# Planning the order of a fused attention and expert kernel anew behind batch 1's scores, with a shorter gate, longer pooling matmuls and another last store

## The chip, the cores and the metric

The kernel runs on one core of a Trainium2 chip. The metric is the device time of one execution in microseconds. Five engines work side by side, each through its own queue in program order: PE (matrix multiplication; its weight loads are shown as PEld), DVE (vector), ACT (scalar and exponential), POOL (masks, and issuing the loads) and SP (issuing the stores). Results of matmuls land in PSUM, which has eight banks of 512 fp32 columns for each of 128 partitions; DVE and ACT copy them out to SBUF. DMA engines move data between SBUF and memory.

## The reference

Eight batches of 576 tokens, in two stages. The first is attention with eight heads of 64, whose keys and values are averaged over eight neighbouring tokens (72 pooled keys). Its output, 512 wide, is `x` of the second stage: four experts with their own 64-wide causal attention, of which every token keeps the two with the largest gate values.

```python
k_p = k.reshape(B, H, Sp, 8, D).mean(axis=3)
v_p = v.reshape(B, H, Sp, 8, D).mean(axis=3)
scores = scale * np.matmul(q, k_p.transpose(0, 1, 3, 2))
...
x = attn_out.transpose(0, 2, 1, 3).reshape(B, S, H * D)
logits = x @ w_gate
topk = np.argpartition(-logits, 2, axis=-1)[..., :2]
...
for e in range(4):
    q, k, v = x @ wq[e], x @ wk[e], x @ wv[e]
    scores = np.where(causal, -1e9, scale * (q @ k.transpose(0, 2, 1)))
    ye = softmax(scores) @ v @ wo[e]
    out += gate weight of e * ye        # for the tokens that chose e
```

Inputs and outputs are fp32; matmuls run on bf16 operands.

## The kernel before

Nothing is scheduled by a compiler. The string `SEQ` (from line 632) lists some 1,140 tokens, and the loop at line 705 carries them out one by one; each engine receives its instructions in that order. A token is a name, arguments, `:batch`, and optionally `@bank`, `d` (the evacuation runs on DVE, else on ACT), `p` (the store is issued by a later token). So `P_k1:2@5` multiplies batch 2's second half of key weights into bank 5, and `p_k1:2d` copies the result out on DVE.

The steps of a batch `b`, by their tokens:

- Loads (POOL, `load`, line 112). `L_k0` to `L_k2`, `L_q0` to `L_q3` and `L_v0` to `L_v2` bring keys, queries and values as bf16 into `kraw`, `qraw`, `vraw`, of which there are three sets, so batch `b + 3` reuses those of `b`. Weights are the tokens `W`; `W4` brings `wop`, the last projection.
- First stage. `PK` (line 265) pools the keys by matmuls with a constant matrix in four strips of 32 partitions side by side; `kc` and `kt` (lines 274, 280) turn the result into `kpT`. `u` turns the queries (`qT`). `E` gives the scores, and `e` (line 320) is their exponential on ACT. `PV`/`vc` pool the values. `D`, `d`, `x` form the reciprocal of the sum; `O` and `o` (DVE, line 365) the output `xT`.
- Second stage, projections. `V`/`v` (line 392) give values and gate logits, `P`/`p` (line 467) queries and keys (`qk`, 512 columns each; `t0` the 64 last tokens of all four, 256 columns).
- Gate. `g0` to `g9` (line 397): exponential on ACT, then the second largest of four logits by larger/smaller of pairs (`hi`, `lo`, two `s`, `m2`), a mask `msk`, the masked weights `W`, their sum, its reciprocal, and the product `G`.
- Second stage, scores. `S` multiplies, `s` (line 490) takes the exponential into `etb` on ACT in four tiles; tile 3, the block of the 64 last tokens, in two instructions (line 497). `a` (line 508) zeroes what lies above the diagonal, on POOL.
- Output. `B` multiplies with the values; `bz`, `bg`, `b` (line 549) divide by the sum and weight by the gate (`osc`, DVE). `T`/`t` turn the result by matmul into `oT`; for batches 2 to 5 the tokens `F` (line 584) do this by a DMA transpose issued by SP. `Y` multiplies with `wop`; `y` (line 602) copies the product to an output tile `ofin`, of which there are nine; `z` and `zs` (line 617) store it. Chunks 0 to 3 are 128 tokens each of one batch; chunk 4 holds the last 64 tokens of two batches together, and is stored in two halves, of which the last of batch 7 goes through ACT's queue. The very last projection, chunk 4 of batch 7, is made and copied in two column halves (`ya4`, `yb4`).

A token whose buffer or bank is still in use waits, and everything behind it on its engine waits too.

Of the kernel before, what the change touches and what calls it, by code (L numbers as in the profile page):

```python
# [16 lines left out]
ISEQ = mybir.AluOpType.is_equal  # L17
EXP = mybir.ActivationFunctionType.Exp
# [3 lines left out]
def kernel(  # L22
# [37 lines left out]
    HALF = TPP // 2  # L60

# [325 lines left out]
    def small(b, nm, *shape):  # L387
        if (b // 2, nm) not in at:
            at[b // 2, nm] = gtp.tile([128, NPC, *shape], FP32, name=nm, tag=nm)
        return at[b // 2, nm]  # L390
# [6 lines left out]
    def gate(b, step):  # L397
# [14 lines left out]
        elif step == 1:  # L412
            L2 = L.rearrange("p c (a b) -> p c a b", b=2)
            for nm, op in (("hi", MAXOP), ("lo", MINOP)):
                nc.vector.tensor_tensor(
                    out=tmp(nm, 2, 1), in0=L2[:, :, :, 0:1], in1=L2[:, :, :, 1:2], op=op
                )
        elif step == 2:
            for nm, src, op in (("s2", "hi", MINOP), ("s3", "lo", MAXOP)):
                nc.vector.tensor_tensor(  # L420
                    out=tmp(nm, 1), in0=got(src)[:, :, 0, :], in1=got(src)[:, :, 1, :], op=op
                )
        elif step == 3:
            nc.vector.tensor_tensor(
                out=tmp("m2", 1), in0=got("s2"), in1=got("s3"), op=MAXOP
            )
        elif step == 4:
            nc.vector.tensor_tensor(
                out=tmp("msk", E), in0=L, in1=got("m2").to_broadcast([128, n, E]), op=ISGE
            )  # L430
        elif step == 5:
            nc.vector.tensor_mul(out=tmp("W", E), in0=got("Ex"), in1=got("msk"))
        elif step == 6:
# [3 lines left out]
        elif step == 7:  # L437
# [4 lines left out]
        elif step == 8:  # L442
# [47 lines left out]
    def sb(b, bank, dve, ep, ti):  # L490
# [4 lines left out]
        if ti == 3:  # L495
            for e in range(2):
                nc.scalar.activation(
                    out=et[half(b), :, e, eo : eo + n],
                    in_=psum[half(b), bank + e, 0 : 2 * n].rearrange("p (a n) -> p a n", a=NEP),
                    func=EXP, scale=MOE_EXP_SCALE,  # L500
                )
# [90 lines left out]
    def Y(b, bank, c):  # L592
        p0 = 128 * place(b, c)
        last = (b, c) == (B - 1, 4)
# [7 lines left out]
    def y(b, bank, dve, c, half=None, later=False):  # L602
        ofin = at[b, "ofin", c] if (b, "ofin", c) in at else ofp.tile([128, DM], FP32, name="ofin", tag="ofin")
        if half is not None:
            cols = slice(256 * half, 256 * half + 256)
            copy(half == 1, ofin[:, cols], psum[:, bank ^ half, cols])
            at[b, "ofin", c] = ofin
            if (b, "half", c) not in at:
                at[b, "half", c] = True
                return  # L610
        else:
            copy(dve, ofin[:], psum[:, bank, :])
        at[b, "ofin", c] = ofin
        if not later:
            z(b, c, nc.sync)

    def z(b, c, queue):
        ofin = at[b, "ofin", c]
        if c == 4:
            for h in range(2):  # L620
                (nc.scalar if h and b == B - 1 else queue).dma_start(
                    out=out[b - 1 + h, MAIN:S, :], in_=ofin[64 * h : 64 * h + 64, :]
                )
        else:
            queue.dma_start(out=out[b, 128 * c : 128 * c + 128, :], in_=ofin[:])
# [10 lines left out]
        H1:0@0c H1:0@0c L_q1:1 H1:0@0c e21:0 e20:0 e11:0 D2:0@4 D0:0@5 L_q2:1 PV:0@6 d0:0 D1:0@7 vc:0d H1:0@0 x0:0  # L636
        c0:0d L_q3:1 d2:0 O00:0@6 d1:0 c1:0d O20:0@5 O01:0@4 o00:0 O10:0@2 x1:0 O11:0@3 o01:0 x2:0 X0:0@0 W2:0 o10:0
        X1:0 o11:0 X2:0 W3:0 c2:0d X3:0 c3:0d o20:0 P_k0:0@4 L_v0:1 h0:0 P_t0:0@5 p_k0:0d L_v1:1 P_k1:0@3 p_t0:0 L_v2:1
        PK:1@2 p_k1:0 S03:0@0 S00:0@4 kc:1 L_k0:2 S02:0@6 s03:0 s02:0 S01:0@2 kt:1d H1:0@0 L_k1:2 H1:0@0 H1:0@0 s01:0
        H1:0@0 L_k2:2 H1:0@0 u1:1 s00:0 u0:1 a02:0 E1:1@02 L_q0:2 e11:1 E0:1@46 c4:0d H1:0@4c L_q1:2 H1:0@4c e00:1  # L640
        V0:0@2 L_q2:2 V1:0@3 e01:1 a00:0 v0:0d V3:0@4 L_q3:2 v1:0d V2:0@2 e10:1 v3:0d a01:0 D1:1@3 v2:0d L_v0:2 PV:1@4
        d1:1 g1:0 E2:1@06 D0:1@2 vc:1d a03:0 x1:1 H1:0@3 L_v1:2 e20:1 g2:0 O11:1@3 e21:1 g3:0 O10:1@4 d0:1 o11:1 D2:1@5
        O01:1@6 L_v2:2 S10:0@0 x0:1 o10:1 S12:0@2 d2:1 s10:0 o01:1 S11:0@4 O00:1@7 g4:0 PK:2@6 s11:0 o00:1 L_k0:3
        O20:1@0 B01:0@1 kc:2 x2:1 B00:0@7 L_k1:3 g0:0 P_q1:1@4 o20:1 kt:2 bz00:0 bz01:0 s12:0 g5:0 L_k2:3 V2:1@0 g6:0
        g7:0 P_q0:1@6 g8:0 L_q0:3 v2:1 u1:2 p_q1:1 P_t0:1@0 a11:0 u0:2 p_q0:1 E1:2@24 L_q1:3 p_t0:1 g9:0 P_k0:1@6
        bg00:0 a10:0 e10:2 b00:0 bg01:0 L_q2:3 b01:0 V0:1@7 e11:2 p_k0:1d a12:0 E0:2@02 v0:1d B10:0@6 L_q3:3 W4:0 e01:2
        V4:1@4 bz10:0 B11:0@7 bg10:0 L_v0:3 b10:0 e00:2 PV:2@5 v4:1d D1:2@6 bz11:0 L_v1:3 P_k1:1@4 vc:2d d1:2 bg11:0
        b11:0 x1:2 E2:2@02 L_v2:3 D0:2@6 p_k1:1d e21:2 O11:2@7 O01:2@5 d0:2 O00:2@2 o11:2 O10:2@4 L_k0:4 e20:2 PK:3@3
        x0:2 o10:2 S03:1@0 S10:1@6 L_k1:4 s03:1 o01:2 s10:1 S01:1@0 o00:2 L_k2:4 V3:1@4 s01:1 kc:3 V1:1@5 L_q0:4 v3:1d
        S02:1@6 S11:1@2 v1:1 kt:3d S12:1@0 s02:1 L_q1:4 V2:2@4 u1:3 P_q1:2@5 a03:1 u0:3 s11:1 L_q2:4 P_q0:2@6 v2:2d  # L650
        s12:1 a02:1 p_q1:2d S00:1@2 L_q3:4 p_q0:2d g0:1 E0:3@04 s00:1 g1:1 L_v0:4 P_k0:2@6 g2:1 e00:3 g3:1 a12:1 g4:1
        P_k1:2@7 p_k0:2d e01:3 L_v1:4 E2:3@02 g5:1 B12:0@6 g6:1 L_v2:4 g7:1 e20:3 B02:0@4 g8:1 e21:3 bz12:0 T10:0@5
        g9:1 p_k1:2 a10:1 E1:3@02 bg12:0 t10:0d L_k0:5 b12:0 bz02:0 B12:1@5 bg02:0 e11:3 b02:0 PK:4@6 L_k1:5 bz12:1
        bg12:1 PV:3@4 b12:1 e10:3 kc:4 S00:2@2 L_k2:5 D1:3@5 vc:3d B01:1@6 s00:2 L_q0:5 kt:4d B02:1@7 T00:0@4 bz01:1
        V1:2@0 d1:3 bz02:1 L_q1:5 bg01:1 bg02:1 T02:0@1 t00:0d T01:0@2 D2:3@3 x1:3 b02:1 D0:3@5 a11:1 b01:1 O10:3@4
        d2:3 O00:3@7 t01:0d d0:3 L_q2:5 D2:2@6 v1:2d T11:0@3 V0:2@2 t02:0 o10:3 x0:3 a01:1 T12:0@5 V3:2@1 u0:4 L_q3:5
        t12:0 v0:2 O20:2@4 O01:3@5 v3:2 O11:3@0 a00:1 o00:3 t11:0 d2:2 L_v0:5 PV:4@1 o11:3 x2:2 x2:3 E0:4@26 o01:3 vc:4
        a00:2 Y3:0@0 L_v1:5 e01:4 o20:2 P_q1:3@5 y3:0dp e00:4 L_v2:5 T12:1@4 u1:4 B10:1@1 P_k1:3@0 p_q1:3 t12:1d bz10:1
        L_k0:6 bg10:1 E1:4@26 b10:1 p_k1:3 g1:2 P_t0:2@5 L_k1:6 e11:4 g2:2 V0:3@4 p_t0:2d Y2:0@0 e10:4 v0:3d Y1:0@5
        y2:0dp L_k2:6 V2:3@4 y1:0p g3:2 E2:4@26 O20:3@0 L_q0:6 v2:3d D1:4@1 e21:4 D0:4@5 o20:3 e20:4 PK:5@4 d1:4 L_q1:6  # L660
        u0:5 S02:2@2 d0:4 S10:2@6 V4:3@1 kc:5 s02:2 B11:1@5 kt:5d P_k0:3@4 v4:3 g4:2 bz11:1 a02:2 s10:2 bg11:1 b11:1
        P_t0:3@1 L_q2:6 p_k0:3d x0:4 T11:1@5 V1:3@0 a10:2 t11:1d p_t0:3 S12:2@2 u1:5 L_q3:6 x1:4 S11:2@4 O01:4@1 s12:2
        v1:3d O11:4@6 P_q0:3@7 o01:4 L_v0:6 s11:2 o11:4 S03:2@0 a12:2 O10:4@2 p_q0:3d D2:4@6 s03:2 PV:5@3 L_v1:6 d2:4
        o10:4 O00:4@4 g0:2 E2:5@06 vc:5 V3:3@5 o00:4 L_v2:6 e20:5 S01:2@2 e21:5 x2:4 v3:3d S01:3@0 a11:2 B00:1@4 s01:2
        g1:3 L_k0:7 T01:1@6 P_k0:4@5 bz00:1 t01:1d bg00:1 s01:3 b00:1 L_k1:7 E0:5@26 p_k0:4d V1:4@4 L_k2:7 e00:5 g2:3
        g5:2 P_k1:4@5 v1:4d L_q0:7 e01:5 g6:2 E1:5@02 g7:2 p_k1:4d V0:4@4 L_q1:7 e10:5 g8:2 T02:1@5 g9:2 P_q0:4@6 a01:2
# [123 lines left out]
```

## Time and profile before

| | before |
|---|---|
| time, median of 3 runs | 154.38 us (154.3 to 154.83) |
| span of the profiled execution, first to last instruction | 152.5 us |
| granted TensorE clock | 0.997 of full |
| PE busy | 140.5 us, 92% |
| ACT busy | 135.1 us, 89% |
| DVE busy | 125.9 us, 83% |
| POOL busy | 89.5 us, 59% |
| stores issued by SP | 32 of 256 KB, 7 of 128 KB, one more of 128 KB by ACT |

The profile comes from one execution. Its own time is known only as the span, which leaves out some 1.9 us around the program that the runs' times contain. A group's row gives line, engine, operation, output and inputs, shapes and count, then busy time, the mean of one instruction in ns, the idle time ahead of the group and what ended it. Busy time counts an overlap of two instructions once; the mean does not, so count times mean can exceed the busy time. A row of the timeline gives start and length in us. A row of DMA issues gives count, size of one and the median us from issue to landing. The row "DMA" shows in forty equal slices of 3.8 us how busy the DMA engines were, in tenths.

### The profile page before, as it was taken

How to read it: one execution, taken by the hardware profiler on the slowest of the kernel's cores; microseconds unless marked ns; L12 is line 12 of the kernel's file. 1: busy time of each engine (PE TensorE's matmuls, PEld its weight loads, DVE VectorE, ACT ScalarE, POOL GpSimd, SP SyncE). 2: the span in 40 equal slices, each digit the busy share in tenths (PEclk: the TensorE clock that was granted, in tenths of full speed). 3: DMA queues.
4: the chain of work that ended last, by engine and by line, in shares of the span. 5: the costliest groups of instructions: out<-in, count | busy, mean ns of one | idle time of the engine just before them, and what ended most of it. 6: DMA issues, size and time to landing. Idle time of an engine off the chain costs nothing.

```text
span 152.5 us, 5419 instructions
## 1 busy us (share of the span) xinstructions
PE 140.5 (92%) x2101; PEld 78.8 (52%) x2122; DVE 125.9 (83%) x415; ACT 135.1 (89%) x247; POOL 89.5 (59%) x161
## 2 busy tenths in 40 slices
PE   6776998999999999999999999999999999999970
PEld 2323353465554465565546655856356667546640
DVE  1784846899899899899989999999897699888960
ACT  3359479999999999999999999999999899999860
POOL 6998588999688979958998171123300344442300
PEclk9999999999999999999999999999999999999998
DMA  4999999999999999999999931536528241389994
GB/s 126 237 186 181 181 179 178 180 180 181 179 188 180 179 181 182 178 180 182 169 173 176 181 34 39 211 84 208 176 92 325 83 121 25 66 282 306 333 340 134
DMA packets 68890, 26.67 MB, mean 175 GB/s; under 512 B 62720, under 2 KB 64000, under 8 KB 68864
## 3 DMA queue, kind: packets, MB, share of 16 engines
q0 software_dynamic: 57408, 14.72, 97.2%
q1 hardware_dynamic: 11088, 10.88, 22.2%
q10 hardware_dynamic: 368, 0.72, 1.5%
q8 instruction: 16, 0.26, 0.6%
q14 instruction: 10, 0.08, 0.2%
HBM read 30.42 MB, written 9.44 MB: 261 GB/s over the span
## 4 chain that ended last, share of the span: by engine, by line
PE 66%; DVE 11%; DMA 10%; POOL 4%; ACT 3%; issue 2%; DVEq 0%; POOLq 0%
PE psum L221 65%; DMA qraw<-in_q_dram 5%; DMA wst_q<-in_moe_wq_dram 4%; DVE xT L377 4%; ACT etb L503 2%; POOL kraw L126 2%; POOL vraw L126 2%; PE psum L230 1%; DVE qT L298 1%; DVE osc L562 1%; DVE oT L212 1%; POOL qraw L126 1%; DVE vp L212 1%; DVE ofin L212 1%; ACT eta L331 1%
## 5 line engine op out<-in xcount | busy, mean ns | idle before, releaser
L503 ACT ACTIVATE etb<-psum 128x1024 bf16<-128x1024 f32 x48 | 47.2, 1032 | 0.8 <-PE psum L221 0.4
L520 POOL TENSOR_SCALAR_AFFINE_SELECT etb<-etb 128x256 bf16<-128x256 bf16 x64 | 25.7, 412 | 37.2 <-ACT etb L503 36.0
L331 ACT ACTIVATE eta<-psum 96x1024 bf16<-96x1024 f32 (+1 forms) x48 | 36.0, 802 | 1.1 <-PE psum L221 0.4
L221 PEld LDWEIGHTS <-etb 128*128 128x128 bf16 x480 | 18.0, 97 | 6.3 <-issue 3.5
L126 POOL DMA_DIRECT2D qraw<-in_q_dram x30 | 19.7, 662 | 2.5 <-DVE gt L557 0.8
L377 DVE TENSOR_TENSOR xT<-psum,rza 128x512 bf16<-128x512 f32 x32 | 20.2, 681 | 1.0 <-ACT rza L354 0.5
L221 PE MATMUL psum<-wvg,xT 128*128 128x260 bf16 x144 | 20.8, 275 | 0.1
L126 POOL DMA_DIRECT2D kraw<-in_k_dram x25 | 19.0, 765 | 2.3 <-POOLq L774 0.8
L221 PE MATMUL psum<-vaug,etb 128*128 128x65 bf16 x480 | 20.2, 193 | 0.0
L126 POOL DMA_DIRECT2D vraw<-in_v_dram x24 | 18.8, 785 | 2.3 <-PE psum L221 1.4
L221 PE MATMUL psum<-xT,wqp 128*128 128x64 bf16 (+1 forms) x123 | 19.2, 282 | 0.5 <-issue 0.2
L221 PE MATMUL psum<-xT,wkp 128*128 128x64 bf16 (+1 forms) x121 | 18.8, 281 | 0.4
L221 PE MATMUL psum<-wop,oT 128*128 128x512 bf16 (+1 forms) x67 | 17.9, 373 | 0.5 <-DVE oT L212 0.3
L212 DVE CAST qk<-psum 128x512 bf16<-128x512 f32 (+1 forms) x23 | 15.0, 653 | 3.6 <-PE psum L221 3.6
L562 DVE TENSOR_TENSOR osc<-psum,gt 128x256 bf16<-128x256 f32 (+2 forms) x40 | 16.7, 421 | 1.0
L221 PE MATMUL psum<-qk 64*128 64x64 bf16 (+4 forms) x192 | 16.2, 277 | 0.6 <-DVE xT L377 0.2
L221 PEld LDWEIGHTS <-xT 128*128 128x128 bf16 x144 | 12.6, 97 | 6.9 <-issue 3.0
L212 ACT COPY ofin<-psum 128x512 f32<-128x512 f32 (+1 forms) x25 | 14.0, 587 | 1.1 <-PE psum L221 0.9
L298 DVE STREAM_TRANSPOSE qT<-qraw 128x576 f32<-128x576 f32 (+1 forms) x18 | 13.2, 750 | 1.0 <-DMA qraw<-in_q_dram 0.9
L221 PE MATMUL psum<-qT,kpT 32*128 32x64 bf16 (+1 forms) x256 | 12.5, 289 | 1.1 <-DVE qT L298 0.9
L221 PE MATMUL psum<-eta,vp 96*32 96x512 bf16 (+1 forms) x256 | 12.7, 288 | 0.5 <-DVE vp L212 0.5
L221 PEld LDWEIGHTS <-wqp 128*128 128x128 bf16 x128 | 8.4, 97 | 8.4 <-issue 2.3
(79 smaller groups left out, 214.4 us busy)
## 6 DMA issues: line engine op xcount, KB each, us to landing
out_dram<-ofin SPq DMA_DIRECT2D x32, 256.0 KB, 2.9
vraw<-in_v_dram POOLq DMA_DIRECT2D x24, 192.0 KB, 6.7
qraw<-in_q_dram POOLq DMA_DIRECT2D x30, 144.0 KB, 7.0
kraw<-in_k_dram POOLq DMA_DIRECT2D x21, 192.0 KB, 7.5
out_dram<-ofin SPq DMA_DIRECT2D x7, 128.0 KB, 2.4
xT<-in_q_dram ACTq DMA_DIRECT2D x2, 288.0 KB, 4.7
xT<-in_k_dram SPq DMA_DIRECT2D x2, 192.0 KB, 4.9
kraw<-in_k_dram POOLq DMA_DIRECT2D x4, 96.0 KB, 5.2
```

The lines of the kernel that those rows point to most:

```text
L126: nc.gpsimd.dma_start(out=dst, in_=src)
L212: (nc.vector.tensor_copy if dve else nc.scalar.copy)(out=out, in_=in_)
L221: nc.tensor.matmul(out=out, lhsT=lhsT, rhs=rhs, start=start, stop=stop)
L230: nc.tensor.transpose(out=out[s], in_=in_[:, s], identity=ident[0:n, 0:n])
L298: nc.vector.transpose(out=dst.rearrange("p (a s n) -> p a n s", s=32, n=n)[:, :, own], in_=src.rearrange("p (a n d) -> p a n d", n=n, d=32 ...
L331: nc.scalar.activation(out=dst, in_=src, func=EXP, scale=ATT_EXP_SCALE)
L377: nc.vector.tensor_tensor(out=xT[:, 2 * got[0][0] + t : 2 * got[-1][0] + t + 1 : 2, m + got[0][1].start : m + got[0][1].stop], in0=psum[:, ...
L503: nc.scalar.activation(out=et[:, ep, :, eo : eo + n], in_=psum[:, bank : bank + 2, 0:n], func=EXP, scale=MOE_EXP_SCALE,)
L520: nc.gpsimd.affine_select(out=blk, in_=blk, pattern=[[0, 2], [1, 128]], compare_op=ISGE, fill=0.0, base=0, channel_multiplier=-1,)
L562: nc.vector.tensor_tensor(out=osc(b, ep)[:, own, :].rearrange("p c (e d) -> p e c d", e=2), in0=o[:, :, :, 0:HD], in1=gt.to_broadcast([128 ...
```

## The change

It has five parts.

1. Pooling of keys: for batches 1 to 7 the three column blocks are one matmul of 384 columns (batch 0 keeps three).
2. Gate: steps 1 to 5 become three. `ahead` compares every logit with every other (bf16 result, 4 by 4 for each token), `c1` counts how many are larger, and one fused operation keeps the exponential where fewer than 1.5 are.
3. Tile 3 of the second stage's scores: one exponential over both banks.
4. The shared chunk 4 is one store of 256 KB. The column halves move from chunk 4 to chunk 3 of batch 7 (`FINAL`), and chunk 4 becomes the last, whole.
5. The order. The tokens up to batch 1's scores are the same; behind `a02:0 E1:1@02` they stand in another order, with other banks and another choice between DVE and ACT. Loads, masks, stores and transposes are moved with it.

```diff
 def PK(b, bank, j=None):
     n = 64 * (own(j).stop - own(j).start)
-    for c in range(3):
+    for cs in [slice(c, c + 1) for c in range(3)] if b in LONG else [slice(0, 3)]:
         for t in range(2):
             for i in range(4):
-                mm(psum[32 * i : 32 * i + 32, bank, n * c : n * c + n], poolk[:, :],
-                   raw[:, c, pair(b, i)][:, own(j), t, :], start=(t == 0), stop=(t == 1))
+                mm(psum[32 * i : 32 * i + 32, bank, n * cs.start : n * cs.stop], poolk[:, :],
+                   raw[:, cs, pair(b, i)][:, :, own(j), t, :], start=(t == 0), stop=(t == 1))
...
         elif step == 1:
-            L2 = L.rearrange("p c (a b) -> p c a b", b=2)
-            for nm, op in (("hi", MAXOP), ("lo", MINOP)):
-                nc.vector.tensor_tensor(out=tmp(nm, 2, 1), in0=L2[:, :, :, 0:1], in1=L2[:, :, :, 1:2], op=op)
+            nc.vector.tensor_tensor(out=tmp("ahead", E, E), in0=L.unsqueeze(2).to_broadcast([128, n, E, E]),
+                                    in1=L.unsqueeze(3).to_broadcast([128, n, E, E]), op=ISGT)
         elif step == 2:
-            for nm, src, op in (("s2", "hi", MINOP), ("s3", "lo", MAXOP)):
-                nc.vector.tensor_tensor(out=tmp(nm, 1), in0=got(src)[:, :, 0, :], in1=got(src)[:, :, 1, :], op=op)
+            nc.vector.reduce_sum(out=tmp("c1", E), in_=got("ahead"), axis=mybir.AxisListType.X)
         elif step == 3:
-            nc.vector.tensor_tensor(out=tmp("m2", 1), in0=got("s2"), in1=got("s3"), op=MAXOP)
-        elif step == 4:
-            nc.vector.tensor_tensor(out=tmp("msk", E), in0=L, in1=got("m2").to_broadcast([128, n, E]), op=ISGE)
-        elif step == 5:
-            nc.vector.tensor_mul(out=tmp("W", E), in0=got("Ex"), in1=got("msk"))
+            nc.vector.scalar_tensor_tensor(out=tmp("W", E), in0=got("c1"), scalar=1.5, in1=got("Ex"),
+                                           op0=ISLT, op1=MULT)
...
         if ti == 3:
-            for e in range(2):
-                nc.scalar.activation(out=et[half(b), :, e, eo : eo + n],
-                    in_=psum[half(b), bank + e, 0 : 2 * n].rearrange("p (a n) -> p a n", a=NEP), ...)
+            nc.scalar.activation(out=et[half(b), :, :, eo : eo + n].rearrange("p a e n -> p e a n"),
+                in_=psum[half(b), bank : bank + 2, 0 : 2 * n].rearrange("p e (a n) -> p e a n", a=NEP), ...)
...
-        last = (b, c) == (B - 1, 4)
+        last = (b, c) == (B - 1, FINAL)
...
         if c == 4:
-            for h in range(2):
-                (nc.scalar if h and b == B - 1 else queue).dma_start(
-                    out=out[b - 1 + h, MAIN:S, :], in_=ofin[64 * h : 64 * h + 64, :])
+            queue.dma_start(out=out[b - 1 : b + 1, MAIN:S, :], in_=ofin[:])
```

The loads behind batch 2's second query load, first as before and then as after, up to batch 4:

```diff
-L_q2:2 L_q3:2 L_v0:2 L_v1:2 L_v2:2 L_k0:3 L_k1:3 L_k2:3 L_q0:3 L_q1:3 L_q2:3 L_q3:3 W4:0 L_v0:3 L_v1:3 L_v2:3 L_k0:4 ...
+L_q3:2 L_q2:2 L_k2:3 L_v1:2 L_v2:2 L_v0:2 L_k0:4 L_q2:3 L_q1:3 L_k1:3 L_k0:3 L_q0:3 L_k1:4 L_q3:3 L_v2:3 L_k2:4 ...
```

SP's queue ahead of the token `y2:2` in the new order, and the end of both orders:

```diff
+y0:3p ... zs0:3 ... zs0:0 ... zs0:2 ... F11:4 ... zs2:1 F00:4 ... Y2:2@3 ... y2:2dp
...
-T12:7@2 t02:7d zs2:7 t12:7d Y4:7@2 zs3:7 ya4:7 yb4:7d
+Y3:7@2 zs0:7 zs1:7 z2:7 t12:6d ya3:7 T02:7@5 t02:7d yb3:7d Y4:7@4 zs3:7 y4:7p zs4:7
```

More of the change, by code (lines that the diff above doesn't have):

```diff
@@ L388, in small @@
         if (b // 2, nm) not in at:
-            at[b // 2, nm] = gtp.tile([128, NPC, *shape], FP32, name=nm, tag=nm)
+            at[b // 2, nm] = gtp.tile([128, NPC, *shape], BF16 if nm == "ahead" else FP32, name=nm, tag=nm)
         return at[b // 2, nm]
@@ L436, in gate @@
             )
-        elif step == 7:
+        elif step == 5:
             nc.vector.scalar_tensor_tensor(
@@ L495, in sb @@
         if ti == 3:
-            for e in range(2):
[L497 to L501, printed above, removed]
+            nc.scalar.activation(
+                out=et[half(b), :, :, eo : eo + n].rearrange("p a e n -> p e a n"),
+                in_=psum[half(b), bank : bank + 2, 0 : 2 * n].rearrange("p e (a n) -> p e a n", a=NEP),
+                func=EXP, scale=MOE_EXP_SCALE,
+            )
         else:
@@ L606, in y @@
             copy(half == 1, ofin[:, cols], psum[:, bank ^ half, cols])
[L607 to L610, printed above, removed]
         else:
             copy(dve, ofin[:], psum[:, bank, :])
-        at[b, "ofin", c] = ofin
-        if not later:
-            z(b, c, nc.sync)
+            if not later:
+                z(b, c, nc.sync)
     def z(b, c, queue):
@@ L642 @@
[L642 to L666, printed above, removed]
```

129 lines of the change are left out of this document (74 added, 55 removed).

## The prediction

> **What bounds the kernel now.** I read the page first, then its chain of waits, then busy time by stage.
>
> ```profile
> span 152.5 us, 5419 instructions
> PE 140.5 (92%) x2101; PEld 78.8 (52%) x2122; DVE 125.9 (83%) x415; ACT 135.1 (89%) x247; POOL 89.5 (59%) x161
> DMA  4999999999999999999999931536528241389994
> PE 66%; DVE 11%; DMA 10%; POOL 4%; ACT 3%; issue 2%; DVEq 0%; POOLq 0%
> 15.00 8.13 DMA qraw<-in_q_dram
> ```
>
> The chain runs through loads until batch 1's queries land at 23.1 us; nothing ahead of that point is reordered. Behind it TensorE carries the chain. The next view splits the rest of the span; its columns are window, length, then busy us of PE, PEld, DVE, ACT and POOL.
>
> ```profile
> 36.00:60.00 24.00, 23.56 (x389) 13.08 (x387) 22.36 (x72) 23.39 (x45) 20.57 (x35) 1.00 1.79 181
> 60.00:90.00 30.00, 29.74 (x457) 15.91 (x456) 28.24 (x87) 29.48 (x56) 22.77 (x40) 1.00 1.69 167
> 90.00:120.00 30.00, 29.58 (x496) 17.94 (x499) 27.04 (x87) 29.47 (x54) 5.55 (x14) 1.00 0.48 154
> 120.00:146.10 26.10, 25.87 (x364) 16.82 (x368) 22.52 (x93) 24.90 (x49) 9.93 (x25) 1.00 0.57 181
> ```
>
> From 36 to 146 us PE idles 1.35 of 110.1 us and ACT 2.86. The two feed each other through eight PSUM banks, so both look full. How full each is shows in the next rows.
>
> ```profile
> 143.58 0.59 PE L221 MATMUL psum<-wop,oT 128*128 128x512 bf16 x2
> L221 PE MATMUL psum<-wop,oT 128*128 128x512 bf16 x63 | 17.3, 380 | 0.2
> L503 ACT ACTIVATE etb<-psum 128x1024 bf16<-128x1024 f32 x48 | 47.2, 1032 | 0.8 <-PE psum L221 0.4
> 119.35 1.94 ACT L503 ACTIVATE etb<-psum 128x1024 bf16<-128x1024 f32 x2 [0.39 <-PE psum L221]
> ```
>
> One 512-column matmul is recorded as 0.38 us, yet two take 0.59: the second starts 0.21 after the first, so up to 0.17 us of waiting behind a PE record still counts as busy. On ACT two exponentials of 1.03 take 1.94, a step of 0.91, so only 0.12 of 1.03 can hide. PE's "full" is the softer one. I take ACT, with PE close behind, as the bound from 60 us on. Before 60 us the DMA row is at 9 throughout: there the loads set the pace.
>
> **The change part by part.**
>
> *Work on ACT.* Counted over the order, these evacuations move from ACT to DVE, net of those moving back: two kpT, two 512-column qk, three 256-column qk, three 64-column oT; one 256-column oT and one ofin come back to ACT. The two 64-partition exponentials of each batch become one.
>
> ```profile
> L212 ACT CAST qk<-psum 128x512 bf16<-128x512 f32 x10 | 5.8, 590 | 0.5 <-PE psum L221 0.5
> L212 ACT CAST qk<-psum 128x256 bf16<-128x256 f32 x5 | 2.0, 408 | 0.3 <-PE psum L221 0.3
> L212 ACT CAST kpT<-kf 128x384 bf16<-128x384 f32 x2 | 1.0, 523 | 0.0
> L212 ACT COPY oT<-psum 128x256 bf16<-128x256 bf16 x5 | 1.9, 388 | 0.4 <-PE psum L230 0.4
> L212 ACT COPY oT<-psum 128x64 bf16<-128x64 bf16 x4 | 0.9, 218 | 0.0
> L212 ACT COPY ofin<-psum 128x512 f32<-128x512 f32 x24 | 13.6, 596 | 0.6 <-PE psum L221 0.4 <-ACT oT L212 0.2
> L497 ACT ACTIVATE etb<-psum 64x128 bf16<-64x128 f32 x16 | 3.5, 271 | 0.1
> L331 ACT ACTIVATE eta<-psum 96x256 bf16<-96x256 f32 x16 | 5.3, 376 | 0.1
> ```
>
> Copies: 2×0.523 + 2×0.590 + 3×0.408 + 3×0.218 − 0.388 − 0.596 = 3.1 us. Exponentials: 16×0.271 − 8×0.376 (priced by the 256-column row) = 1.3. Together 4.4 us of records in 16 fewer instructions. Each neighbour hides about 0.12 of a record, so the time freed may be as little as 4.4 − 16×0.12 = 2.5. Since ACT runs back to back, I take 2.5 and keep 4.4 for the range. About 0.5 of it lies ahead of 60 us, where loads pace the work; 2.0 is left.
>
> *Work on DVE.* It receives the copies and loses part of the gating.
>
> ```profile
> L212 DVE CAST qk<-psum 128x512 bf16<-128x512 f32 (+1 forms) x23 | 15.0, 653 | 3.6 <-PE psum L221 3.6
> L212 DVE CAST kpT<-kf 128x384 bf16<-128x384 f32 (+1 forms) x6 | 3.0, 502 | 0.1
> L428 DVE TENSOR_TENSOR msk<-L,m 128x16 f32<-128x16 f32 (+1 forms) x8 | 1.6, 201 | 0.1
> L420 DVE TENSOR_TENSOR s<-lo 128x4 f32<-128x4 f32 (+1 forms) x8 | 1.3, 158 | 0.0
> L562 DVE TENSOR_TENSOR osc<-psum,gt 128x128 bf16<-128x128 f32 x8 | 2.2, 288 | 0.2
> ```
>
> Copies add at most 5×0.653 + 2×0.502, less the ofin that leaves (0.596, ACT's row): 3.7. Seven small operations per batch (hi, lo, two s, m, msk, W) go: 56 at 0.16 to 0.20, 9 to 11.2 us. Three come back (compare of 64 or 80 elements, sum, fused threshold): 24 between the 0.201 of msk and the 0.288 of a 128-element product, 4.8 to 6.9; I take 0.25, 6.0. DVE ends between +1.6 and −2.7 us, about even. It idles 9.9 of the 110.1 us above, which covers even +1.6; without that cover this 1.6 would come off the gain.
>
> A page prices the new compare directly. The Trainium skill, "VectorE: DVE Perf Modes", section on the TRN2 errata, gives a two-input fp32 operation (N+151)/0.96 ns, 224 to 241 ns here (an estimate by that page); with it the added gating is some 5.6 us instead of 6.0 and the sum stays. The trace agrees only roughly: for 16 to 20 elements the formula gives 174 to 178 ns, msk's row 201.
>
> *Pooling matmuls.* For batches 1 to 7 twenty-four 128-column matmuls become eight of 384 columns, with as many columns streamed.
>
> ```profile
> 43.11 0.51 PE L221 MATMUL psum<-kraw,poolk 96*32 96x128 bf16 x24
> 54.30 0.40 PE L221 MATMUL psum<-vraw,poolv 96*32 96x512 bf16 x3
> ```
>
> Today 24 take 0.51. The nearest long form is one group of side-by-side strips of 512 columns, 0.40; with a second start 0.21 later, two groups take 0.61. By columns (384 of 512) that is 0.46, and if only the spacing shrinks, 0.40 + 0.16 = 0.56. So a batch gains 0.05 or loses 0.05, seven batches ±0.4. I take −0.1: as many columns are streamed and 16 weight loads fewer.
>
> *Loads.* The same 79 loads; the queue's order changes behind batch 2's second query load.
>
> ```profile
> qraw<-in_q_dram POOLq DMA_DIRECT2D x8, 144.0 KB, 7.3
> 37.90 0.66 POOL L126 DMA_DIRECT2D qraw<-in_q_dram  x1
> 46.49 1.42 DVE L298 STREAM_TRANSPOSE qT<-qraw 128x576 f32<-128x576 f32 x2
> 49.42 0.63 PE L221 MATMUL psum<-qT,kpT 32*128 32x512 bf16 x8
> ```
>
> The loading stages move 181 GB/s, so a key load of 192 KB holds the DMA engines for 1.06 us. Two such loads of batch 4 (L_k0:4, L_k1:4) now stand ahead of batch 3's last query load. That one was issued at 37.90 and landed about 7.3 later, at 45.2; with 2.1 us more ahead of it, 47.3. The two transposes that read it began at 46.49, so DVE would wait up to 0.8 there, with v2:2 and p_q0:2 queued behind. The scores that need them began at 49.42, 1.5 after the transposes ended. I price this at 0 by that cover; without it, it costs the 0.8. Two stores (zs3:0, zs2:0) enter the loading stage, near 66 us, where batch 5's loads follow; a store's 256 KB at 181 GB/s would push them 1.4 us each at most. Weights wop slip behind batch 4's loads.
>
> *Tail.* Chunk 3 of batch 7 is evacuated in halves, and the shared last tokens follow whole.
>
> ```profile
> 148.16 0.42 DVE L212 COPY ofin<-psum 128x256 f32<-128x256 f32 x1 [0.74 <-PE psum L221]
> 148.66 0.55 ACTq L621 DMA_DIRECT2D out_dram<-ofin  x1
> out_dram<-ofin ACTq DMA_DIRECT2D x1, 128.0 KB, 2.6
> out_dram<-ofin SPq DMA_DIRECT2D x1, 256.0 KB, 2.0
> out_dram<-ofin SPq DMA_DIRECT2D x32, 256.0 KB, 2.9
> ```
>
> The last copy grows from 0.42 to ACT's 0.60 for a whole tile (+0.18), the landing from issue falls from 2.6 to the 2.0 of a lone 256 KB store (−0.6), or to the page's median 2.9 (+0.3) if queued. Bounds −0.4 to +0.5; I take 0.
>
> *Sum.* −2.0 (ACT), 0 (DVE), −0.1 (pooling), 0 (loads, tail): 152.5 − 2.1 = 150.4 of span. The span lies 1.9 below the 154.38 median of three runs, so the time is 152.3.
>
> **The rivals.** *PE is the bound.* For it: PE's idle is the smaller of the two, and the chain is 66% PE. Against: its records hide up to 0.17 us each. ACT's relief is then worth nothing, only pooling's −0.4 to +0.4 counts and a little of the order: 154.2.
>
> *Loads pace longer.* For it: the DMA row stays at 9 up to 87 us. If relief counts only behind that, half of the 2.0 is lost: 153.3. Against: PE idles less from 60 to 90 us (0.26 of 30) than from 36 to 60 (0.44 of 24).
>
> *Output tiles run out (slower).* There are nine output tiles; a new one waits until the store nine before it has landed. In the new order y2:2 on DVE needs the store of y2:1, only fifteen tokens ahead, and SP gets to that one after three stores and a transpose.
>
> ```profile
> 95.58 1.55 SPq L625 DMA_DIRECT2D out_dram<-ofin  x3
> 97.22 2.13 SPq L587 DMA_TRANSPOSE oT<-osc  x1
> 106.83 1.22 SPq L590 DMA_TRANSPOSE oT<-osc  x1
> ```
>
> From y0:3's copy, which frees SP: 3×0.52 + 1.22 to 2.13 + landing 2.0 to 2.9 from the issue of y2:1's store = 4.8 to 6.6 us. ACT's work between that copy and Y2:2 is at least the four large exponentials of batch 5 (0.91 each), two small (0.27) and one qk copy (0.59), 4.8. DVE would wait up to 1.8 us, with bz11:5 and bz01:5 behind it and their PSUM banks held. Two more close pairs follow (y1:4, y3:4). It decides once the store lands more than 4.8 after that copy; two waits of the full 1.8 cost 3.6, and from the forecast 152.3 the time is 155.9. Against: 2.0-us landings are seen too.
>
> **How the numbers follow.** Forecast 152.3: 0.48, its own range 150.5 (ACT's 4.4 less 0.5 ahead of 60 us, nothing else) to 153.5 (the two bad bounds of loads and pooling, 0.8 and 0.5). Loads 0.12. PE 0.16. Output tiles 0.24. A measurement tells about 0.5% (0.8 us) from no change. Faster takes the first and most of the second, 0.58; same the third and the second's rest, 0.18; slower 0.24. The range goes from 150.5 to 155.8, which leaves no more than two in ten outside.
>
> **What would show it.** Right: ACT's busy time down by about 4 us with its share still 97% or more between 60 and 140 us; DVE's within 3 us of 125.9; a pooling group of eight in about 0.5; batch 3's query transposes near 46.5; PE's last Y4 about 2 us earlier. Wrong: DVE ofin waiting for a DMA (output tiles); ACT's share falling with PE's at 99% (PE bound); POOL waiting for ACT's etb ahead of 80 us with gaps in the DMA row, which would starve loads and make this forecast too low.

## The result and the profile after

| | before | after |
|---|---|---|
| time, median | 154.36 us (4 runs) | 171.21 us (4 runs, 170.08 to 173.02) |
| span of the profiled execution | 152.5 us | 170.9 us |
| granted TensorE clock in it | 0.997 | 0.959 |

The ratio is 1.106, interval 1.1015 to 1.1105: slower by about 16.9 us where 2.1 us of gain was forecast. Medians here and below are of all runs, while a ratio compares only those within 1.5% of the fastest run of their kernel. The profiled execution of after took 173.02 us; the spans of the other three are 167.9 to 169.3 us.

First the page of after: span, busy time, the DMA row in forty slices of 4.3 us, the chain by engine, and the median from issue to landing of the stores.

```profile
span 170.9 us, 5136 instructions
PE 146.1 (86%) x2010; PEld 78.6 (46%) x2010; DVE 122.9 (72%) x391; ACT 133.4 (78%) x231; POOL 88.7 (52%) x161
DMA  5999999999999999999997773962064557676810
PE 42%; DMA 28%; ACT 10%; DVE 6%; issue 4%; SPq 3%; POOL 1%; DVEq 0%; ACTq 0%; POOLq 0%
out_dram<-ofin SPq DMA_DIRECT2D x35, 256.0 KB, 6.5
```

ACT and DVE are busy 1.7 and 3.0 us less than before. TensorE has fewer matmuls and yet 5.6 us more of busy time. Of this, 1.5 us are there without the merged store as well (142.0 us in the run in two halves below). For the rest, its granted clock is below full in two stretches that begin near the ends of two waits: 0.50 from 114 to 116 us and 0.57 from 156.5 to 160. Why it falls there isn't shown; behind a third wait, of 2.1 us until 148.5, it stays full. The chain has 28% in DMA where it had 10%, and a store takes 6.5 us to land where it took 2.9. Next the stages of after, in the columns of the view of before (window, length, busy us of PE, PEld, DVE, ACT, POOL, then granted clock, DMA share, GB/s).

```profile
36.00:60.00 24.00, 23.71 (x342) 12.28 (x343) 22.31 (x71) 23.31 (x41) 20.54 (x35) 1.00 1.66 167
60.00:90.00 30.00, 28.98 (x428) 15.10 (x417) 26.80 (x75) 27.56 (x56) 20.54 (x35) 1.00 1.61 171
90.00:120.00 30.00, 27.71 (x424) 15.52 (x424) 23.69 (x76) 25.39 (x42) 8.54 (x20) 0.94 0.64 91
120.00:146.10 26.10, 26.10 (x370) 16.29 (x363) 21.04 (x77) 24.16 (x39) 9.89 (x26) 1.00 0.49 143
146.10:171.00 24.90, 8.75 (x96) 5.24 (x92) 5.88 (x29) 7.82 (x17) 0.00 (x0) 0.79 0.51 182
```

Up to 60 us the stages are as before. TensorE loses 1.0 of 30 us from 60 to 90, where it waits for batch 5's values, and 2.3 from 90 to 120, and then needs 24.9 us for the last 8.75 us of its work. The chain of waits from 100 us on, with start, length and engine, names what it waits for.

```profile
106.95 5.39 DMA oT<-osc
112.38 29.13 PE psum L224 x393
...
145.58 10.79 DMA out_dram<-ofin
156.47 0.59 ACT ofin L215
...
160.51 0.62 PE psum L224 x2
161.15 0.59 ACT ofin L215
```

Two waits stand out: a transpose that lands 5.4 us after its issue, and a store that takes 10.8 us, behind which ACT waits for an output tile. The list of waits (total, times, longest) has the same, and SP's timeline says which stores these are: L608 is the shared last tokens' store, L610 a whole tile's.

```profile
ACT ofin L215 <- DMA out_dram<-ofin: 6.8, 2, 4.4
PE psum L224 <- ACT oT L215: 3.9, 1, 3.9
```

```profile
101.76 0.68 SPq L608 DMA_DIRECT2D out_dram<-ofin  x1
102.50 1.11 SPq L579 DMA_TRANSPOSE oT<-osc  x1
...
145.58 1.35 SPq L608 DMA_DIRECT2D out_dram<-ofin  x1
147.03 14.16 SPq L610 DMA_DIRECT2D out_dram<-ofin  x12
161.76 0.54 SPq L608 DMA_DIRECT2D out_dram<-ofin  x1
```

Both delays begin at a merged store of the last tokens (101.76, 145.58). The last one (161.76) stands alone at the end, so its pace can be read off the DMA view of 161.7 to 171 us, whose forty slices are 0.23 us each.

```profile
DMA  9992111111111111010111111111111110000000
GB/s 361 388 370 79 44 53 53 44 53 53 53 53 44 53 44 44 26 53 35 53 53 53 53 53 44 53 53 44 53 53 53 53 53 35 0 0 0 0 0 0
```

For three slices the whole tiles issued before it run at 361 to 388 GB/s with the engines at nine tenths; then one tenth of the sixteen engines is busy, at 53 GB/s, until 169.6 us. That fits two engines of sixteen (53 of 388 GB/s is 0.14), and it is 7.8 us from issue instead of the 2.3 to 2.6 of the two halves before. The written access is 2 by 64 by 512: its outermost dimension is 2. The Trainium skill, "DMA: Bandwidth & Descriptors", section "Why a DMA increments its semaphore by 16 and not by 1", says that a transfer is spread over the largest number of engines up to 16 that divides the outermost dimension of both sides, here 2 against 128 partitions. The row above agrees, with 53 of 388 GB/s, and so does the third run below.

### The profile page after: what moved, and what is told of

It is laid out like the page before. It is cut to its first block, busy times and chain, and to the rows that moved or that the text cites. A ratio compares the mean times of both kernels' runs of the same rounds, so it can differ in the third digit from the quotient of the medians.

```text
span 170.9 us, 5136 instructions
## 1 busy us (share of the span) xinstructions
PE 146.1 (86%) x2010; PEld 78.6 (46%) x2010; DVE 122.9 (72%) x391; ACT 133.4 (78%) x231; POOL 88.7 (52%) x161
## 4 chain that ended last, share of the span: by engine, by line
PE 42%; DMA 28%; ACT 10%; DVE 6%; issue 4%; SPq 3%; POOL 1%; DVEq 0%; ACTq 0%; POOLq 0%
PE psum L224 41%; DMA out_dram<-ofin 6%; DMA vraw<-in_v_dram 6%; DMA qraw<-in_q_dram 5%; DMA wst_q<-in_moe_wq_dram 4%; DMA kraw<-in_k_dram 3%; DMA oT<-osc 3%; ACT etb L495 3%; DVE xT L380 2%; ACT eta L334 2%; ACT ofin L215 2%; DVE qT L301 1%; ACT rza L357 1%; SPq L582 1%; PE psum L233 1%
## 5 line engine op out<-in xcount | busy, mean ns | idle before, releaser
L512 POOL TENSOR_SCALAR_AFFINE_SELECT etb<-etb 128x256 bf16<-128x256 bf16 x64 | 24.6, 406 | 31.1 <-ACT etb L495 30.8
L224 PE MATMUL psum<-wop,oT 128*128 128x512 bf16 (+1 forms) x74 | 21.3, 393 | 2.5 <-DMA oT<-osc 2.2
L215 ACT COPY ofin<-psum 128x512 f32<-128x512 f32 (+1 forms) x26 | 14.7, 586 | 8.8 <-DMA out_dram<-ofin 6.8
L215 DVE CAST qk<-psum 128x512 bf16<-128x512 f32 (+1 forms) x28 | 17.4, 627 | 4.9 <-PE psum L224 3.9
L224 PE MATMUL psum<-xT,wkp 128*128 128x512 bf16 (+1 forms) x128 | 20.1, 294 | 0.0
L224 PE MATMUL psum<-xT,wqp 128*128 128x64 bf16 (+1 forms) x128 | 19.7, 286 | 0.0
L547 DVE RECIPROCAL rzb<-psum 128x4 f32<-128x4 f32 (+2 forms) x40 | 6.9, 176 | 9.3 <-PE psum L224 8.3
L215 DVE CAST vaug<-psum 128x256 bf16<-128x256 f32 x26 | 10.9, 419 | 3.6 <-PE psum L224 3.1
```

Of the source, the lines that this page charges most:

```text
L215: (nc.vector.tensor_copy if dve else nc.scalar.copy)(out=out, in_=in_)
L224: nc.tensor.matmul(out=out, lhsT=lhsT, rhs=rhs, start=start, stop=stop)
L512: nc.gpsimd.affine_select(out=blk, in_=blk, pattern=[[0, 2], [1, 128]], compare_op=ISGE, fill=0.0, base=0, channel_multiplier=-1,)
L547: nc.vector.reciprocal(out=rz, in_=o[:, :, :, HD : HD + 1])
```

## The experiments

The kernel before was run beside each; its medians there lie between 154.30 and 154.74 us. "The new order in two halves" is the kernel after with the store undone.

**The merged store alone: undone, and done in the old order.**

```diff
-            queue.dma_start(out=out[b - 1 : b + 1, MAIN:S, :], in_=ofin[:])
+            for h in range(2):
+                (nc.scalar if h and b == B - 1 else queue).dma_start(
+                    out=out[b - 1 + h, MAIN:S, :], in_=ofin[64 * h : 64 * h + 64, :])
```

> The changed kernel with the shared last tokens stored in two halves again, as before; all else of the change stays. Theory A: the one store of 256 KB runs through two of the sixteen DMA engines, because the slowest dimension of its destination has size 2 (the trace of the changed kernel shows its packets one after the other until 7 us after the issue), and what is queued behind it waits; with halves nearly all of the 17 us goes and the sum of the prediction is left, 151.5 to 154.5 us. Theory B: the new order runs out of output tiles and of loads by itself; then 160 us or more.

Measured 157.28 us (155.99 to 160.51), ratio 1.0168, interval 1.0126 to 1.0210. Of 16.9 us, 13.9 are gone; 3 stay, which neither theory had. With them it is still outside the predicted range, whose upper end is 155.8. In its profile no copy of an output tile waits for a store any more: the group of these copies has 1.3 us of idle time ahead of it where after had 8.8.

```profile
L215 ACT COPY ofin<-psum 128x512 f32<-128x512 f32 (+1 forms) x26 | 14.5, 587 | 1.3 <-ACT ofin L215 0.8
```

The same edit the other way round, in the kernel before:

> The kernel before, its order kept, with the shared last tokens in one store of 256 KB as its only change. Theory A: the last store alone needs some 7.5 us from issue to landing instead of 2.6, so at least 154.4 + 4.9 = 159.3 us, up to 166 where the three earlier ones hold back stores and transposes. Theory B: 154 to 155, since a store less is issued each time.

167.61 us, ratio 1.0819 (1.0762 to 1.0875): 13 us dearer with nothing else changed, and more than the 166 that theory A had as its upper end. Its page has the wait for the output tiles, in the kernel whose order had none:

```profile
L212 ACT COPY ofin<-psum 128x512 f32<-128x512 f32 (+1 forms) x25 | 14.1, 587 | 6.6 <-DMA out_dram<-ofin 5.6
out_dram<-ofin SPq DMA_DIRECT2D x36, 256.0 KB, 4.7
```

**One transfer on sixteen engines.** The rows of a batch pair alternate in the output tile (the columns of `oT` are written with a stride of 2), so the one store of batches 0/1 and 6/7 is 64 by 2 by 512. Batches 2 to 5 keep halves.

```diff
+        dst = oT[:, MAIN + o : MAIN + 128 : 2] if part is not None and p0 == 4 else oT[:, c0 : c0 + n]
...
+            if b in (1, B - 1):
+                queue.dma_start(out=out[b - 1 : b + 1, MAIN:S, :].rearrange("h s d -> s h d"), in_=ofin[:])
```

> As e1, but for batches 0 and 1 and for 6 and 7 the rows of the shared chunk alternate between the two batches, so that one store of 256 KB has a slowest dimension of 64 in its destination (128 rows in its source); batches 2 to 5 keep halves. Theory A (the number of DMA engines, not the single transfer, is what costs): the single store lands within 2.0 to 2.9 us of its issue, and the time is that of e1 within 0.7 us. If one transfer over two blocks of memory is slow in itself: 4 us or more above e1.

157.22 us, ratio 1.0182 (1.0152 to 1.0211), the same as two halves. From 149.8 to 154 us its DMA view has:

```profile
DMA  9999999999999999999999999941010000000000
GB/s 332 371 429 371 351 449 332 371 390 371 410 390 410 351 332 429 429 371 390 371 390 371 390 410 351 449 176 59 20 39 0 0 0 0 0 0 0 0 0 0
...
out_dram<-ofin SPq DMA_DIRECT2D x1, 256.0 KB, 3.6
```

The engines run at nine tenths and 330 to 450 GB/s until the last packets. The two interleaved stores land 2.9 and 3.6 us after their issue. That is later than the 2.0 to 2.9 expected, but about as late as the last two halves in the run with two halves (3.3 and 3.7). So one transfer instead of two costs nothing here, and the few engines are what cost the 14 us.

**The other parts in the old order.** The shorter gate, the 384-column pooling and the fused exponential are put into the kernel before, with its order and its two stores.

> The kernel before with its order, its choice of engines and its stores, and with the pooling matmuls of 384 columns, the shorter gate (in the places of the old steps) and the one exponential for tile 3. Frees about 0.5 us on ACT, 4 us on DVE and at most 0.4 on PE. If ACT or PE bound the order: 153.8 to 154.4. If DVE's gate steps were in the way: 152 to 153.5. Slower than 155 would mean that one of the new forms costs more than its rows say.

154.67 us, ratio 1.0016 (1.0001 to 1.0032): the same. Its page, and the pooling group's row of it:

```profile
PE 142.2 (93%) x2010; PEld 77.4 (51%) x2010; DVE 122.7 (80%) x383; ACT 134.7 (88%) x239; POOL 89.5 (59%) x161
L223 PE MATMUL psum<-kraw,poolk 96*32 96x384 bf16 x56 | 3.6, 328 | 0.0
```

DVE has 3.2 us less to do, ACT 0.4, TensorE 112 weight loads and as many matmuls fewer, and the time doesn't fall; it lies just above the 154.4 that the expectation had for a bound on ACT or PE. So the rest of the 3 us goes with the order. This takes in its banks, its choice between DVE and ACT and the column halves at the end, which no run takes apart.

**Where the order's 3 us lie: the loads.** In the new order two stores of batch 0 are issued at 62.5 and 66.7 us, while batch 5's loads are under way. The DMA issues from 62 to 75 us (count, size, median us to landing), of the new order in two halves and then of before:

```profile
vraw<-in_v_dram POOLq DMA_DIRECT2D x4, 192.0 KB, 8.8
kraw<-in_k_dram POOLq DMA_DIRECT2D x3, 192.0 KB, 8.9
out_dram<-ofin SPq DMA_DIRECT2D x2, 256.0 KB, 6.3
qraw<-in_q_dram POOLq DMA_DIRECT2D x3, 144.0 KB, 8.8
```

```profile
vraw<-in_v_dram POOLq DMA_DIRECT2D x5, 192.0 KB, 5.5
kraw<-in_k_dram POOLq DMA_DIRECT2D x3, 192.0 KB, 7.4
qraw<-in_q_dram POOLq DMA_DIRECT2D x4, 144.0 KB, 6.4
```

Loads land 1.5 to 3.3 us later after their issue. Four runs tried to get this back, all on the new order in two halves.

```diff
-zs3:0 g2:2 zs2:0 O20:3@4
+g2:2 O20:3@4
...
+zs1:0 zs3:0 zs2:0
```

> The new order with the last tokens in two halves (157.28 us), and the two early stores of batch 0's output tiles 3 and 2, which stood at 62.5 and 66.7 us between batch 5's loads, moved back to about 95 us. Open are the 3 us by which the new order stays above the kernel before (154.3). Theory L (the loads of batch 5 come just in time: they land 0.06, 0.19 and -0.44 us ahead of their first use, where the kernel before had 4.0, 1.1 and 3.95; TensorE falls 1.1 us behind between 60 and 80 us): without the two stores these loads land 1 to 2 us earlier and the time falls by 0.5 to 1.0 us, to 156.3 to 156.8. Theory Q (the DMA transposes of batch 2 stand too late in SyncE's queue, at 102 to 112 us): unchanged or up to 0.6 us worse, as two stores more stand ahead of these transposes, 157.2 to 157.9. Theory E (the new order has more of the output stores at the end, 28 behind 130 us where the kernel before has 24, and these come 0.65 us apart): unchanged, 157.1 to 157.5.

160.12 us, ratio 1.0237 (1.0171 to 1.0304): no gain; whether it is worse than two halves the overlapping intervals leave open. The loads do land sooner (6.6 to 7.2 us), batch 5's values 1.7 us ahead of their use. But at 95 us the two stores meet the last three loads, two of batch 7's queries and one of its values, which the new order issues only there. The values land at 103.2 us, and TensorE stands:

```profile
PE psum L224 <- DMA vraw<-in_v_dram: 2.3, 1, 2.3
```

All three theories missed this. The loads in the order of before, in the new order's places:

> The new order with the last tokens in two halves (157.28 us); the loads stand at the same places of GpSimd's queue, but in the order of the kernel before, batch by batch, so that batch 5's stand up to four places earlier. Theory L: batch 5's loads land 1 to 3 us earlier, TensorE loses 0.5 to 1.0 us less between 60 and 80 us: 156.3 to 156.8. Theories Q and E: 157.0 to 157.5, as neither the transposes nor the last stores move.

158.51 us, ratio 1.0227 (1.0175 to 1.0279). Batch 5's loads now land 2.1 to 3.4 us ahead of use, as theory L has it, and no time is gained. Both edits together:

> Both at once: the two stores moved back and the loads batch by batch. Theory L: all of the 1.1 us between 60 and 80 us comes back, 156.0 to 156.5. Theory Q: 157.0 to 157.8. Theory E: 157.0 to 157.5.

160.18 us, 1.0224 (1.0158 to 1.0291), with 1.5 us of waiting for batch 7's values and 0.5 for batch 4's. And with the stores between the transposes moved behind them:

> As the run before it, and the stores of batch 0/1's last tokens (two halves) and of batch 1's tile 3, which stand between the transposes of batches 2 and 3 at 100.8 to 105.1 us, moved behind these transposes. Theory Q: the transpose that the product of batch 2's tile 3 waits for (landed 109.9, TensorE idle 0.8 to 1.0 us) is issued 1.8 us earlier, the wait is gone: 0.6 to 1.0 us below the run before it. Theory E: the same as the run before it within 0.3 us, since the end is paced by the stores. Theories L and Q together would leave 155.2 to 155.8, still above 154.3, and the rest would be E's.

159.91 us, 1.0302 (1.0253 to 1.0350). The wait for the transposes is gone, but 1.7 us of waiting for batch 7's values and 0.8 for batch 4's stay, so Q is not decided by it. The next two take the late values away:

```diff
-F11:2 L_v0:7 b00:3 ... L_v1:7 L_v2:7 B10:3@1
+L_q3:7 L_v0:7 L_v1:7 L_v2:7
```

> The new order with the last tokens in two halves; the loads batch by batch, and the last three of them (batch 7's values, issued at 94.3 to 95.8 us in the run with loads batch by batch, landing 0.6 us behind their first use) issued at about 86 us. In the runs with the two stores moved back these three loads landed 2.1 to 2.8 us late and TensorE stood 1.7 to 2.5 us before batch 7's PK. Theory L2 (what the stores moved back cost came from these three loads): they land by 96 us, no wait at batch 7; the time is 0 to 0.5 us below the run with loads batch by batch (158.5 on its chip, 157.3 in its fastest profile), 156.5 to 157.5. Without L2: unchanged.

157.37 us, 1.0164 (1.0134 to 1.0195): no wait for batch 7's values, and no faster than the two halves. The two early stores behind the last load as well:

> As the run before it, with the two early stores of batch 0 (62.5 and 66.7 us) behind the last load, at about 88 us, as the kernel before has its first stores behind its last load. Theory L (loads and stores must not share the stretch in which loads come just in time): no wait at batch 5 nor at batch 7, 155.8 to 156.6, the last store's late landing (1.0 us) and TensorE's rest of 0.5 us being left above 154.3. Theory E alone: 156.8 to 157.5.

157.39 us, 1.0161 (1.0132 to 1.0190). Theory L is refuted as the main cause: with batch 5's and batch 7's loads in time 2.7 of the 3 us stay.

**Where they lie: the end.** Lighter stores there, first of batches 5 and 6, then of 6 and 7, each with a control in the old order.

```diff
-            queue.dma_start(out=out[b, 128 * c : 128 * c + 128, :], in_=ofin[:])
+            n = 64 if b in (5, 6) else 128
+            queue.dma_start(out=out[b, 128 * c : 128 * c + n, :], in_=ofin[:n, :])
```

> The new order with the last tokens in two halves (157.28 us, span 155.0 in its profile), and the stores of the whole tiles of batches 5 and 6 write 64 of their 128 rows: 1 MB of the output is left out, with the instructions, the waits and the order as they were. Theory E (the end is paced by the stores: in the new order the last two land 3.35 and 3.66 us after their issue, in the kernel before 2.3 and 2.6): the last stores land 2.3 to 2.7 us after their issue, the time falls by 0.7 to 1.2 us, to about 156.1 to 156.6. Rival W (only TensorE's waits count, the stores land late but cost nothing that the next issue would not): 157.0 to 157.6.

157.69 us, 1.0190 (1.0155 to 1.0226): no gain, and the last stores still land 3.2 to 4.0 us after issue.

> The kernel before, with the stores of the whole tiles of batches 5 and 6 writing 64 of their 128 rows: 1 MB of the output is left out. Control for the light end of the new order. Theory E: the kernel before gains nothing or little, 153.9 to 154.5, as its last stores land 2.3 and 2.6 us after their issue, as quick as a lone one. If it gains 0.7 us or more, the stores pace the end of both kernels and the light end tells nothing of the new order.

154.42 us, 0.9987 (0.9969 to 1.0004).

> The new order with the last tokens in two halves; now the whole tiles of batches 6 and 7 are stored with 64 of their 128 rows, 1 MB of the output left out. In the run that lightened batches 5 and 6 the queue was empty by 148 us (2.2 us from issue to landing), and five whole tiles' worth of batch 7 were then issued within 2.3 us (148.3 to 150.6), which at 0.63 us per 256 KB is 3.1 us: that run lightened the wrong stores. Theory E: the last two land 2.2 to 2.7 us after their issue in place of 3.2 to 4.0, and the time is 1.0 to 1.5 us below the new order in two halves (157.3), 155.8 to 156.4. Rival W: no gain, 157.0 to 157.7.

156.99 us, 1.0142 (1.0098 to 1.0186), the last stores at 3.3 to 3.6 us. With half the rows the engines were still at seven to nine tenths, at 180 to 290 GB/s most of the time: the test was weak.

> The kernel before with the same light stores of batches 6 and 7, the control. Theory E: 154.0 to 154.6, no gain beyond 0.3 us, as its last stores land 2.3 and 2.6 us after issue. If it falls by 0.8 us or more, the stores pace both ends alike and say nothing of the new order.

154.37 us, 0.9992 (0.9974 to 1.0010).

> The new order with the last tokens in two halves, with the loads batch by batch and the last three early, and the light stores of batches 6 and 7 together. Theories L and E as a sum: TensorE ends 0.3 to 0.6 us earlier than in the two-halves run and the last store lands 1.0 to 1.5 us sooner, 155.2 to 156.2. If it is no better than the light end alone, the loads had no price; if it stays above 157, neither is the cause of the rest.

156.57 us, 1.0109 (1.0068 to 1.0150). That is above the 155.2 to 156.2 expected of both theories together. The last three runs:

```diff
-zs0:7 zs1:7 z2:7 t12:6d
+zs0:7 zs1:7 zs2:7 t12:6d
```

> The new order with the last tokens in two halves (157.28 us); the store of batch 7's tile 2, which the change issues on ScalarE's queue (148.67 us), goes on SyncE's queue as in the kernel before. In all profiles of the new order, with full and with light stores, the landings have a gap of 1.1 to 1.6 us at this store (151.25 to 152.46 us in the two-halves run) and all later stores land 3.2 to 4.0 us after their issue. Theory Z (a whole tile on the second queue among the last stores holds them up): the last stores land 2.3 to 3.0 us after their issue, 0.5 to 1.0 us gained, 156.2 to 156.8. Rival: the gap is the queue of stores itself, no gain, 157.0 to 157.6.

157.65 us, 1.0192 (1.0142 to 1.0242): theory Z falls.

> The new order with the last tokens in two halves and all that helped or may help: loads batch by batch with the output weights' load behind batch 4's values as the new order has it, the last three loads early, the store of batch 7's tile 2 on SyncE's queue. Theory L with theory Z: TensorE's wait of 0.9 to 1.5 us behind batch 4's PV in the runs with loads batch by batch is gone, 155.4 to 156.4. If neither counts: 157.0 to 157.6.

156.64 us, 1.0117 (1.0069 to 1.0165), the least of all versions of the new order that store everything. Without the stores of batches 5 and 6:

```diff
-        else:
+        elif b not in (5, 6):
```

> As the run before it, and the whole tiles of batches 5 and 6 are not stored at all: 2 MB of the output is left out. The light stores of 64 rows kept the DMA engines 85 to 90% busy at the end at half the bytes, so they were a weak test. Theory E in its strong form: with nothing queued ahead the last stores land 2.3 to 2.7 us after their issue, 1.0 to 1.5 us below the run before it, 154.3 to 155.4. If it gains less than 0.5 us, the stores at the end are not what keeps the new order above the kernel before, and TensorE's later end is.

156.17 us, 1.0106 (1.0060 to 1.0151). By the medians 0.5 us, with overlapping intervals; by the profiles more. The last product on TensorE and the last stores of the run before it, then of this run (the timeline's start and length; the DMA issues' median to landing), spans 155.0 and 153.4 us:

```profile
148.09 0.60 PE L224 MATMUL psum<-wop,oT 128*128 128x512 bf16 x2 [0.29 <-DVE oT L215]
...
out_dram<-ofin ACTq DMA_DIRECT2D x1, 128.0 KB, 3.2
out_dram<-ofin SPq DMA_DIRECT2D x1, 128.0 KB, 3.8
```

```profile
148.23 0.61 PE L224 MATMUL psum<-wop,oT 128*128 128x512 bf16 x2 [0.28 <-DVE oT L215]
...
out_dram<-ofin SPq DMA_DIRECT2D x1, 128.0 KB, 2.3
out_dram<-ofin ACTq DMA_DIRECT2D x1, 128.0 KB, 2.6
```

TensorE ends no earlier. What differs is the stores' way out: the last one is issued at 149.53 for 150.11 us and lands 2.6 us after it for 3.8. So in these two executions the crowded end is worth 1.6 us of span. TensorE's own end in the run with all stores is 0.6 us later than before:

```profile
147.47 0.60 PE L221 MATMUL psum<-wop,oT 128*128 128x256 bf16 x4 [0.28 <-DVE oT L212]
```

The profile of the two halves shows where its 3 us lie. Its last product starts 1.45 us later than the kernel before's:

```profile
148.92 0.61 PE L224 MATMUL psum<-wop,oT 128*128 128x512 bf16 x2 [0.28 <-DVE oT L215]
```

From there to the end of the span it takes 6.1 us, before 5.0, so another 1.05. The remaining 0.5 us lie outside the span: time less span has a median of 2.2 to 2.3 us in every run that keeps the new order of the loads, 1.7 to 1.9 with the loads batch by batch, and 1.7 in the kernel before. Why the order of the loads should matter there is not shown.

What causes the 3 us is not settled to better than this: some 0.6 us for loads and queues together (157.3 to 156.6, intervals overlapping), 0.5 to 1.6 for the stores at the end, and the rest open. The run with the best queues takes 155.5 to 157.6 us in five of its six runs, the kernel before beside it 154.2 to 155.2. Why the new order spreads was not found. No version that stores everything was faster than the kernel before.

## Why the prediction was wrong

*Tail: this step failed.* It priced the landing of the merged store at "the 2.0 of a lone 256 KB store" or "the page's median 2.9", with bounds of −0.4 to +0.5. Both rows are of whole tiles, 128 rows by 512 on both sides. The merged store has the size but not the shape; it moved at the pace of two DMA engines and took 7.8 us. The step also saw one store where there are four. The first delayed the transposes of batch 2 (TensorE waits 2.2 us until 112.4, and 0.8 in two halves), the next two held output tiles (ACT waits 2.4 and 4.4 us), the fourth ends the span 5 us late. Undoing it took back 13.9 us, doing it in the old order cost 13.3.

*The order: a second step failed.* Beside the tail, the sum had −2.0 for ACT and 0 for the loads. With the store undone the time is 3 us above the kernel before, where these terms put it 2 below, and TensorE's last product comes 1.45 us later, not 2 earlier. ACT's relief came and bought nothing (below). A price for the new places of loads and stores was left at 0; the runs showed some 0.6 us for the loads and queues and 0.5 to 1.6 for more stores at the end, and the cause of the rest stays open.

*Output tiles run out.* The wait that this rival named as its sign came (ACT's, not DVE's), but not by its price: in the run in two halves the stores land a median of 3.6 us after their issue, later than the 2.0 to 2.9 of the rival's sum, and still no copy waits for a tile. It was a consequence of the tail.

*ACT.* Of 4.4 us of records, 2.5 were taken as freed; the page shows 1.7 (135.1 to 133.4), so the sign of about 4 us less failed. Added up one by one, ACT's records are 4.3 us shorter, so the count was right; 2.6 of it had been overlap, where the step took 1.9. The size freed is near, but the claim that ACT is the bound is not borne out. In two halves the stages are:

```profile
60.00:90.00 30.00, 29.68 (x412) 15.21 (x408) 27.09 (x75) 27.93 (x57) 20.64 (x36) 1.00 1.66 176
90.00:120.00 30.00, 29.18 (x476) 17.33 (x473) 26.57 (x83) 28.54 (x48) 8.13 (x19) 1.00 0.45 85
120.00:146.10 26.10, 26.10 (x375) 16.83 (x371) 21.11 (x85) 24.57 (x41) 9.89 (x26) 1.00 0.68 220
```

From 60 to 90 us ACT is busy 1.55 us less than before and TensorE's busy time stays (29.74 to 29.68); from 120 on ACT has 94% and TensorE all of it. What was taken from ACT became idle time on ACT. That is the sign given for the rival "PE is the bound". It is not proof of it: as the prediction says, waiting behind a PE record counts as busy, and from 90 to 120 us TensorE has 97%. The run with the other parts in the old order does not test its 154.2 either, since it takes only 0.4 us from ACT.

*DVE.* "About even", between +1.6 and −2.7: the page has −3.0 (125.9 to 122.9), just outside. The three new operations take 0.16 to 0.26 us each, some 5.0 us in all where 6.0 were taken; the sum also leaves out the copies of `oT` that its own count moves, 0.3 us by ACT's rows. In the old order 3.2 us less on DVE gained nothing, as the step had it.

*Pooling.* Eight matmuls of 384 columns took 3.6/7 = 0.51 us for a batch in the old order, as the twenty-four did; −0.1 was taken. (In after the groups take 4.1 us, because two of the seven stand among other matmuls and spread over 0.76 and 0.80; the others take 0.50 to 0.51.)

*Loads.* Batch 3's last query load lands at 47.3 us in after, as worked out, but partly by luck: it is issued 2.8 us later than before (40.69 for 37.90) and takes 6.6 us for 7.6. The transposes come at 48.48 and 50.32 us, not near 46.5. The first scores need only one of them. It ends at 49.25 us where it ended at 47.91, and these scores start 0.43 us later, held last by an exponential:

```profile
48.48 0.77 DVE L301 STREAM_TRANSPOSE qT<-qraw 128x576 f32<-128x576 f32 x1
49.85 0.63 PE L224 MATMUL psum<-qT,kpT 32*128 32x512 bf16 x8 [0.18 <-ACT etb L495]
```

DVE waits for no load there, so the cover held but for these 0.43 us. The two stores push batch 5's loads as bounded, by 1.1 us each: batch 5's values land at 73.96 with them and at 71.80 without, for two. That taking them away gains nothing was not foreseen. (By its own terms the forecast's upper bound is 153.6, not 153.5.)

## What to carry to other kernels

Price a transfer by its shape, not by its bytes: use as a row for it only one with the same outermost dimension on both sides, and where the trace has none, bound it by the bytes over the pace of the few engines that it may get. A slow store isn't late alone: transposes and the stores that free output tiles land late behind it, so four of them, of which the last costs 5 us at the end, cost 14 in all. And work taken from a nearly full engine need not shorten anything: here ACT went from 98% to 93% from 60 to 90 us while TensorE stayed at 99%.

## What the runs showed of the hardware

One store of 256 KB with an outermost dimension of 2 moved at 53 GB/s with one tenth of the sixteen DMA engines busy; with an outermost dimension of 64 the same bytes, as one transfer, left the engines at nine tenths and 330 to 450 GB/s in all. With four such slow stores among them, the median landing of the 256 KB stores went from 3.6 to 6.5 us in the new order and from 2.9 to 4.7 in the old. And storing half of the rows did not halve what the stores take of the engines: at the end, 64 rows a tile kept them at seven to nine tenths, mostly at 180 to 290 GB/s, where 128 rows had them at nine tenths and mostly 350 to 400.
